# A fused attention and GEGLU kernel: new turns for its operations, other buffers for the last stores, another split of the last block

## The chip, the cores and the metric

The kernel runs on one core of a Trainium2 chip. The metric is device time in microseconds (us) of one execution; before the change the median of three runs is 225.25 us (225.17 to 226.1). Five engines work side by side, each through its own list of instructions in order: PE (TensorE, matrix products), DVE (VectorE), ACT (ScalarE), POOL (GpSimd) and SP, which here only issues DMA transfers.

## The reference

An input of 2048 rows by 448 columns, bfloat16, goes through a layer norm; an attention with memory and a gated feed-forward layer both read the result:

```python
xn = _layernorm(x, axis=-1)
s = _A_ref(xn, A_wq, A_wk, A_wv, A_wo, A_beta)
g = _silu(_B_ref(xn, B_w_gate, B_w_up, B_w_down))
return x + s * g
```

`_B_ref` is `_gelu(x @ w_gate) * (x @ w_up) @ w_down` with 1792 hidden columns. `_A_ref` has 16 heads of 28 and walks over four segments of 512 rows:

```python
for s in range(N):
    logits = jnp.einsum('bhqd,bhkd->bhqk', qs, ks) * scale + mask
    p = _softmax(logits, axis=-1)
    a_dot = jnp.einsum('bhqk,bhkd->bhqd', p, vs)
    pq = phi(qs)                       # t+1 where t>0, else exp(t)
    num = jnp.einsum('bhld,bhde->bhle', pq, M)
    den = jnp.einsum('bhld,bhd->bhl', pq, z)[..., None] + 1e-06
    outs.append(g * (num / den) + (1.0 - g) * a_dot)
    M = M + jnp.einsum('bhld,bhle->bhde', phi(ks), vs)
    z = z + jnp.einsum('bhld->bhd', phi(ks))
```

The joined outputs are multiplied by `wo`.

## The kernel before

The 2048 rows are four segments, each of four blocks of 128 rows. For a segment the kernel normalises the blocks, transposes them (in segment 0 on PE, later by DMA transposes from SP), projects q, k and v, computes scores and exponentials (sc, ex, mk), the products with v (pv), the read of the memory (rd) and its update (up). The feed-forward layer of a segment has 14 chunks of 128 hidden columns: PE computes gate and up of a chunk, ACT the GELU into one of three small buffers `gl` (line 1007), DVE the product of the two into `hT` (line 1012), which frees the two PSUM banks of the chunk for PE. Four chunks can have banks at a time. The down projection (dn), the output projection (wo), SiLU (th), the product of both (fm) and the residual (fa, line 1076) finish a block; SP stores it (st).

Segment 0 is special in three ways. Its gate and up products run in two halves, gi (through line 969, four column pieces) and gu (three pieces), where gu of a chunk has to follow the GELU of the chunk before it, or, for the first three chunks, a tiny ACT copy tg. Its q rows wait for their transposes in the slots of `hT` that chunks 8 to 11 write later, so hm08 to hm011 follow the transposes tq00 to tq03. And while its 14 chunks run, DVE also normalises segment 1 (bn, ag, ep, xn, du), and sums squares of the weights for a guard (rq).

All operations are made as named objects; a table, `TURNS`, lists all names in the order in which they are recorded, and so sets the order on every engine: a name in it is an operation, with the segment as first digit and chunk, block or step behind it (hm03: segment 0, chunk 3; st31: segment 3, block 1). The planner `arrange` checks that each name follows what it depends on and picks buffers; it changes no turn. DMA transfers go through SP in this order too, and each waits for the transfer eight before it in the program.

The last segment's blocks finish one by one: down projection, SiLU on ACT, output projection, product on DVE, residual into one of two buffers `oo`, store. The last block (b = 3) is cut in two column parts, each with its own chain; the first part's store is issued by SP, the second's by ACT. The buffer `wo_sb` of the output weights, 128 x 1792, is zeroed before the four transfers wo_in fill 28 of each 32 rows.

Of the kernel before, what the change touches and what calls it, by code (L numbers as in the profile page):

```python
# [89 lines left out]
x00 x02 x01 wv wk wv2 warm warm_up wv3 wk2 qs2 ident va0 kn0 nhalf table bn00 su2 ag00 xc0 su3 va1 wk3 wq wq2  # L90
wq3 beta wgh ez1 kn1 xc_z trc00 bn01 ag01 wuh wg0 wu0 wg4 wu4 xc2 evc00:ACT trc02 xc1 xc3 trc01 trc03 evc02:ACT
wv00 ep00 wv02 ep01 evc01:DVE evc03:DVE qs0 pw00 xn00 du00 wv03 tr00 sv3 sv2 ep03 qs3 red_z ep02 wv01 wr0 pw01
wk00 vb0 qs1 pw03 vb1 ones ez0 pw02 sq0 sq1 xn01 ev00:DVE evwv02:DVE wk02 evwv00:DVE evwv03:DVE du01 evwv01:DVE
xn03 sq2 x1 wk01 wk03 wr1 sq3 evwk02:DVE xn02 du03 evwk00:ACT evwk03:DVE wg8 evwk01:ACT wq02 wq03 du02 tr01
exwk00 ev01:DVE wq00 tr03 tr02 gates sq4 ev03:DVE wq01 wr2 ev02:DVE gi00 gi01 tk00 tk03 qs4 evwq01:ACT
evwq00:DVE evwq03:DVE evwq02:DVE wu8 tg00 exwk01 rq0 bn10 gi02 gu00 ag10 bn12 tg01 ag12 bn11 ag11 miwk01 ge00
tg02 gu01 hm00 bn13 ag13 ep10 miwk00 pw10 ge01 sq5 tq00 tq03 sq6 gi03 gu02 tk02 hm01 ge02 hm02 xn10 xn12 du10
rq1 bd bd0 tr10 gi04 gu03 ge03 gi05 gu04 ge04 xn13 hm03 gi06 du13 gu05 hm04 ge05 gi07 gu06 ge06 gi08 gu07 tr13
ge07 sq7 x2 tq01 hm05 xn11 gi09 gu08 phwk01 rq2 du11 du12 ge08 hm06 gi010 tr11 tq02 gu09 hm07 ge09 gi011 hm08
rq6 rq5 hm09 bn20 gi012 rq3 ag20 bn21 bn23 gu010 ge010 gi013 wd_in1 gu011 gu012 ge011 ag23 hm010 tk01 hm011  # L100
gu013 ge012 ge013 bd1 wk10 hm012 wk11 wr1wk0 hm013 evwk10 wo0 ag21 bn22 sc00 wq11 wd_in0 wv10 ex000 ag22 evwk11
rq4 ex001 wq10 tr12 wr1wq0 evwq10 ep20 sc01 ex010 wv11 pw20 evwq11 wr1wv0 evwv11 evwv10 sc02 xn20 xn22 xn23
ex011 mk011c384 xn21 dn000 ex020 ex021 wo_in1 mk020c0 mk021c0 bd2 mk021c256 mk001c0 sc03 mk000c0 dn005 ex030
ex031 mk031c0 mk010c0 mk011c0 x3 mk010c384 wq13 du20 phwk00 sc04 ex040 dn0010 tk10 bn30 rq7 ex041 bn31 up0 tk11
bn33 wq12 tq10 mk020c256 tq11 ag30 ag33 gates2 mk041c384 mk040c0 mk040c384 sc05 wr1wq2 macc th00 sg00 ex050
mk041c0 ex051 ag31 mk050c0 evwq13 ux tr20 bn32 exwk10 mk030c0 mk051c0 tr23 tr22 wk12 wk13 wr1wk2 evwk13 tr21
pv02 ag32 evwk12 sc06 ep30 evwq12 tq13 ex060 dn010 ex061 miwk10 sc07 dn015 ou000 ex070 pv04 sc08 phwk10 pw30
ex071 ou010 tk13 tq12 ex080 xn30 dn0110 mk060c0 dn020 th01 sc09 ex081 mk070c256 mk061c0 xn31 gx mk071c256 ex090
ex091 tk12 den000 xn32 mk071c0 mk070c0 mk060c384 xn33 du30 sg01 exwq10 den010 dn025 mk061c384 pv07 dn0210 nrm
sc10 wv12 mk080c0 bd3 mk081c0 ou020 mk090c384 tr30 ex100 ex101 den020 mk090c0 mk091c0 mk091c384 pv09 nrm2 wv13  # L110
ou030 wr1wv2 sc11 evwv12 evwv13 den030 tr31 th02 ex110 ex111 dc00 wk20 wk21 wv20 wr2wk0 mc0 miwq10 sg02 sc12
ex120 tr32 tr33 wv21 phwq10 evwk21 evwk20 wr2wv0 mk101c0 wv23 mk111c0 evwv20 wv22 wr2wv2 ex121 exwq11 sc13 dg00
dn030 rc00 evwv23 evwv22 ex130 mk110c384 rd003 mk110c0 mk120c0 mk121c256 mk121c0 mk120c256 miwq11 evwv21 rd002
rd000 rd001 wq32 rd11 wq33 wo_in0 wr3wq2 rb000 rb020 rb010 ex131 wo_in2 rb030 wo_in3 sc14 phwq11 exwk11 miwk11
mk100c0 ou111 ex140 ex141 mk140c384 evwq32 dn035 rd10 rd13 xw10 xw11 mk141c384 mk130c0 dn0310 th03 mk141c0
mk111c384 mk131c0 mk140c0 evwq33 rd12 sc15 ou101 ou131 ex150 ou121 cb00 sg03 wk22 phwk11 wk23 wr2wk2 pv12 ex151
den121 evwk22 den101 cb02 evwk23 sc16 cb01 den111 den131 ex160 ex161 wq21 wq20 up1 wr2wq0 sc17 ou100 evwq21
evwq20 pv14 wq22 tq20 tk20 den100 ou110 ex170 ex171 cb03 wq23 wr2wq2 evwq22 um1 sc18 tq22 den110 ex180 dc11
mk171c256 wo02 fm02 wo01 mk161c384 wo00 ex181 fm01 sc19 mk170c0 mk151c0 mk170c256 ex190 gu10 mk181c0 evwq23 tq23
# [1491 lines left out]
```

## Time and profile before

| what | value |
|---|---|
| median of three runs | 225.25 us (225.17 to 226.1) |
| the profiled execution's own time | 225.96 us |
| its span, first to last instruction | 224.2 us |
| granted TensorE clock | 0.997 |
| PE busy | 215.8 us, 96% of the span |
| DVE, ACT, POOL busy | 157.5, 159.7, 126.4 us |
| PE busy in the first and the last 8 us | 6.35 and 3.17 us |
| DMA | 27.71 MB, 124 GB/s on the mean |

The profile's times count from the first instruction of the span. PE's matmuls are pipelined: one of 512 columns is recorded as about 380 ns, while the next starts some 215 ns after it. So a stall of PE shows as a longer distance between two starts, and as idle time only where it is longer than the pipeline. "[0.47 <-DVE hT L1012]" behind a row means that the engine was idle for 0.47 us before it, and that this write of `hT` at line 1012 ended the wait.

### The profile page before, as it was taken

What the parts mean: (1) busy time and instruction counts of PE and PEld (TensorE: products, weight loads), DVE (VectorE), ACT (ScalarE), POOL (GpSimd) and SP (SyncE); (2) the same over time, 40 slices, a digit from 0 to 9 for tenths busy, and PEclk for the clock granted to TensorE, in tenths of its full rate; (3) what the DMA queues carried; (4) which work ended last, traced back from release to release, by engine and by line L of the source; (5) the groups of instructions that cost most, each with busy time, mean ns of one, the idle gap of its engine ahead of it and who ended that gap; (6) DMA issues with size and microseconds to landing.
All of it is one profiled execution on the core that took longest, in us unless ns stands there. A gap on an engine that the chain in (4) does not pass through costs nothing. (4 is left out here: it accounts for less than half of the span.)

```text
span 224.2 us, 5093 instructions
## 1 busy us (share of the span) xinstructions
PE 215.8 (96%) x1896; PEld 97.8 (44%) x1896; DVE 157.5 (70%) x289; ACT 159.7 (71%) x214; POOL 126.4 (56%) x219
## 2 busy tenths in 40 slices
...
GB/s 181 240 338 195 174 131 241 287 148 160 143 66 83 128 207 79 84 61 164 35 195 169 116 49 47 45 125 109 136 153 0 28 53 26 132 90 228 1 44 53
DMA packets 45463, 27.71 MB, mean 124 GB/s; under 512 B 30664, under 2 KB 40840, under 8 KB 45432
## 3 DMA queue, kind: packets, MB, share of 16 engines
...
q10 hardware_dynamic: 1216, 0.97, 1.4%
q8 instruction: 17, 0.28, 0.6%
...
## 5 line engine op out<-in xcount | busy, mean ns | idle before, releaser
L861 ACT ACTIVATE pt<-pp 128x1024 bf16<-128x1024 f32 x76 | 73.9, 1026 | 12.3 <-PE pp L846 11.9
L872 POOL TENSOR_SCALAR_AFFINE_SELECT pt<-pt 128x256 bf16<-128x256 bf16 x128 | 52.7, 445 | 13.9 <-ACT pt L861 13.6
L1055 PE MATMUL ps<-wd_sb,hT 128*128 128x448 bf16 x196 | 41.7, 353 | 0.2 <-DVE vaug L615 0.2
L1012 DVE TENSOR_TENSOR hT<-gl,ps 128x512 bf16<-128x512 bf16 x28 | 19.0, 683 | 17.6 <-ACT gl L1007 17.6
L999 PEld LDWEIGHTS <-wg_sb 64*128 64x128 bf16 x252 | 23.1, 94 | 15.1 <-issue 1.7
L999 PEld LDWEIGHTS <-wu_sb 64*128 64x128 bf16 x252 | 23.2, 94 | 14.5
L1012 DVE TENSOR_TENSOR hT<-gl,pp 128x512 bf16<-128x512 bf16 x28 | 18.6, 679 | 13.6 <-ACT gl L1007 12.5
L1055 PEld LDWEIGHTS <-hT 128*128 128x128 bf16 x210 | 19.1, 98 | 20.0 <-issue 4.2
L1007 ACT ACTIVATE gl<-ps 128x512 bf16<-128x512 f32 x28 | 16.6, 597 | 15.5 <-PE ps L999 8.4
L1007 ACT ACTIVATE gl<-pp 128x512 bf16<-128x512 f32 x28 | 16.1, 596 | 13.9 <-PE pp L999 10.2
L770 POOL TENSOR_TENSOR om<-om,rb 128x512 f32<-128x512 f32 x12 | 14.9, 1266 | 17.0 <-DMA rb<-rdr 17.0
L579 PEld LDWEIGHTS <-xnT 128*128 128x128 bf16 (+1 forms) x192 | 14.5, 96 | 21.1 <-issue 12.2
L694 POOL TENSOR_SCALAR e<-e 128x896 bf16<-128x896 bf16 (+1 forms) x12 | 11.8, 986 | 20.9 <-ACT e L689 12.5
L817 POOL TENSOR_TENSOR oT<-oa,om 128x512 bf16<-128x512 f32 x12 | 15.9, 1329 | 6.3 <-DVE oa L814 6.3
L511 POOL TENSOR_TENSOR rs<-rs,nhalf 128x1 f32<-128x1 f32 (+1 forms) x7 | 5.3, 756 | 24.3 <-DVE rs L506 24.0
L999 PE MATMUL ps<-xnT,wg_sb 64*128 64x512 bf16 x66 | 17.9, 377 | 0.0
L999 PE MATMUL ps<-xnT,wu_sb 64*128 64x512 bf16 x66 | 17.8, 376 | 0.0
L999 PE MATMUL ps<-xn,wu_sb 64*128 64x512 bf16 x66 | 17.8, 376 | 0.0
L999 PE MATMUL ps<-xn,wg_sb 64*128 64x512 bf16 x66 | 17.8, 376 | 0.0
L846 PE MATMUL pp<-qT,kT 32*128 32x384 bf16 (+3 forms) x244 | 16.5, 300 | 0.0
L999 PE MATMUL pp<-xnT,wg_sb 64*128 64x512 bf16 x60 | 16.2, 376 | 0.0
L999 PE MATMUL pp<-xnT,wu_sb 64*128 64x512 bf16 x60 | 16.2, 376 | 0.0
(132 smaller groups left out, 457.2 us busy)
## 6 DMA issues: line engine op xcount, KB each, us to landing
...
```

What stands on the lines that cost most here:

```text
L511: o = gps(f"pw{s}{bs[0]}", 0.97 if s else 0.56, lambda r=r: nc.gpsimd.tensor_tensor(out=rs.ap()[:, r], in0=rs.ap()[:, r], in1=nhalf[:, r], ...
L579: nc.tensor.matmul(out=self.bank.ap()[:, 0:D], lhsT=self.xT.ap()[r, c, n * P:(n + 1) * P], rhs=self.w[r, c, :], **kw)
L694: o = gps(f"mi{nm}{s}{half}", n / 1024, lambda: nc.gpsimd.tensor_scalar(out=t(), in0=t(), scalar1=1.0, scalar2=0.0, op0=ALU.min, op1=ALU.max),
L770: oU[s, g, 1] = t, gps(f"sm{s}{g}", 1.22, lambda t=t, r=r: nc.gpsimd.tensor_tensor(out=t.ap(), in0=t.ap(), in1=r.ap(), op=ALU.mult), deps= ...
L817: oT[s][1].append(gps(f"cb{s}{g}", 1.22, lambda g=g, t=t, tm=tm: nc.gpsimd.tensor_tensor(out=dst.ap()[:, g, :], in0=t.ap(), in1=tm.ap(), o ...
L846: nc.tensor.matmul(out=S2[i // 2].ap(i % 2)[:, c0:c0 + n], lhsT=kT[s][0].ap()[r, g, kb * P:(kb + 1) * P], rhs=qT[s][0].ap()[r, g, kb * P:L ...
L861: nc.scalar.activation(out=dst, in_=src, func=ACT.Exp, scale=scale)
L872: nc.gpsimd.affine_select(out=v, in_=v, pattern=[[0, 2], [1, P]], compare_op=ALU.is_ge, fill=0.0, base=0, channel_multiplier=-1)
L999: nc.tensor.matmul(out=bf[fc].ap(i), lhsT=w, rhs=x, start=c == 0, stop=c == 2 * NC3)
L1007: got[fc] = nc.scalar.activation(out=gl.ap(), in_=bf[fc].ap(0), func=ACT.Gelu_apprx_tanh)
L1012: nc.vector.tensor_tensor(out=hT[s][0].ap()[:, fc, :], in0=gl.ap(), in1=bf[fc].ap(1), op=ALU.mult), deps=[a] + held,
L1055: nc.tensor.matmul(out=bank.ap()[:, 0:D], lhsT=hT[s][0].ap()[:, fc, b * P:(b + 1) * P], rhs=wd_sb[:, fc, :], start=(fc == 0), stop=(fc == ...
```

## The change

Four edits, and a new table:

- `wo0`, the zeroing of `wo_sb`, moves from POOL to DVE.
- The transfer of `beta` is issued after x1 (segment 1 of the input), no longer ahead of the gate and up weights.
- In the last segment the residual sums go to the three GELU buffers `gl`, no longer to the two `oo`.
- The last block is cut at column 320, no longer at 256: 320 and 128 columns instead of 256 and 192.
- `TURNS` is replaced as a whole. On PE both tables are much alike; POOL, DVE, ACT and SP are ordered anew in many places.

```diff
@@ the table, a few of its rows @@
-fm32 wo30 dn330a wo31 dn3110 fa32:DVE fm30 dn335a dn3310a wo330 fa30:DVE dn335b dn3310b st32 th31 st30 fm31
-fa31:DVE st31 th330 y330 fa330:DVE st330 th331 wo331 y331 fa331:DVE st331
+th32 wo30 th30 fm30 wo31 dn330a wo32 st21 fa30:POOL fm31 st30 fa31:POOL st31 dn335a dn3310a wo330 dn330b dn335b
+dn3310b wo331 fm32 th330 fa32:DVE th331 st32 y330 fa330:DVE st330 y331 fa331:DVE st331
...
-        beta_in = load("SP", "beta", betac[:], A_beta.rearrange("(h o) -> h o", o=1).unsqueeze(1)
-                       .to_broadcast([H, RC, 1]), 2)
...
                 x_in[1] = [load("SP", "x1", xs[1][:], x_v[1], 448)] * NB
+                beta_in = load("SP", "beta", betac[:], A_beta.rearrange("(h o) -> h o", o=1).unsqueeze(1)
+                               .to_broadcast([H, RC, 1]), 2)
...
-        wo_z = fill("POOL", "wo0", 1.55, -70, wo_sb[:], 0.0)
+        wo_z = fill("DVE", "wo0", 0.6, -70, wo_sb[:], 0.0)
...
         def finish(s, b, pr):
-            bank, oo = Buf(B_, END if s == LAST else ONE), Buf(oo_p)
+            bank, oo = Buf(B_, END if s == LAST else ONE), Buf(gl_p if s == LAST else oo_p)
...
-            dma(f"st{s}{b}", 112, lambda: nc.sync.dma_start(out=o_v[s][:, b, :], in_=oo.ap()),
+            dma(f"st{s}{b}", 112, lambda: nc.sync.dma_start(out=o_v[s][:, b, :], in_=oo.ap()[:, 0:D]),
...
         def last_block(pr):
-            t, oo, parts, last = Buf(sg_p), Buf(oo_p), [slice(0, 256), slice(256, D)], []
+            t, oo, parts, last = Buf(sg_p), Buf(gl_p), [slice(0, 320), slice(320, D)], []
```

The first place is DVE where segment 0's chunks begin. L619 of `hT` is the eviction of a q block, L493 a bn of segment 1, L1012 a chunk's product hm, L1149 a sum of squares rq. Before:

```order
L619 TENSOR_SCALAR hT<-ps_92,rs_143 128x16x28
L1149 TENSOR_REDUCE red<-pt_108 128x16
L493 BN_STATS st_139<-x_sb_64 128x6
L495 BN_AGGR mv_142<-st_139 128x2
L493 BN_STATS st_140<-x_sb_64 128x6
L495 BN_AGGR mv_142<-st_140 128x2
L493 BN_STATS st_137<-x_sb_64 128x6
L495 BN_AGGR mv_142<-st_137 128x2
L1012 TENSOR_TENSOR hT<-gl_128,pp_91 128x512
```

With the change:

```order
L389 MEMSET wo_sb 128x896
L1149 TENSOR_REDUCE red<-pt_108 128x16
L619 TENSOR_SCALAR hT<-ps_95,rs_143 128x16x28
L619 TENSOR_SCALAR hT<-ps_93,rs_143 128x16x28
L619 TENSOR_SCALAR hT<-ps_94,rs_143 128x16x28
L493 BN_STATS st_139<-x_sb_64 128x6
L493 BN_STATS st_140<-x_sb_64 128x6
L1012 TENSOR_TENSOR hT<-gl_128,pp_90 128x512
L1012 TENSOR_TENSOR hT<-gl_129,pp_91 128x512
L493 BN_STATS st_137<-x_sb_64 128x6
```

Two bn instead of three stand ahead of the first product, and no ag; the zeroing of `wo_sb` and an rq stand ahead of the three evictions of q.

The second place is SP at the same time: transposes of k and q of segment 0, and the loads of the last gate and up columns (128x3x768). Before:

```order
L351 DMA wg_sb<-in_B_w_gate_dram 128x3x768
L628 DMA_TRANSPOSE kT_102<-kn_86 128x4x128 x2
L351 DMA wu_sb<-in_B_w_up_dram 128x3x768
L628 DMA_TRANSPOSE qT_100<-hT 128x4x128 x2
L628 DMA_TRANSPOSE kT_102<-kn_86 128x4x128
L550 DMA_TRANSPOSE xnT_99<-xn_96 128x4x128 x2
L425 DMA x_sb_65<-in_A_x_dram 128x4x448
L628 DMA_TRANSPOSE qT_100<-hT 128x4x128
```

With the change:

```order
L628 DMA_TRANSPOSE kT_102<-kn_86 128x4x128 x3
L628 DMA_TRANSPOSE qT_100<-hT 128x4x128
L351 DMA wg_sb<-in_B_w_gate_dram 128x3x768
L351 DMA wu_sb<-in_B_w_up_dram 128x3x768
L628 DMA_TRANSPOSE qT_100<-hT 128x4x128 x2
L628 DMA_TRANSPOSE kT_102<-kn_86 128x4x128
L628 DMA_TRANSPOSE qT_100<-hT 128x4x128
L550 DMA_TRANSPOSE xnT_99<-xn_96 128x4x128 x2
L425 DMA x_sb_65<-in_A_x_dram 128x4x448
```

All four transposes of q now stand ahead of segment 2's input (x_sb_65) and of those of segment 1; both weight loads stand behind four transposes instead of none and two.

The third place is DVE at the end: L1093 is fm, L1076 the residual fa, L1129 the product y of a part of the last block, L1176 the read of the guard's flag. Before:

```order
L1093 SCALAR_TENSOR_TENSOR sg_134<-sg_134,ps_95 128x448
L1076 TENSOR_TENSOR oo_136<-sg_134,x_sb_66 128x448
L1129 SCALAR_TENSOR_TENSOR sg_133<-sg_133,ps_92 128x256
L1076 TENSOR_TENSOR oo_135<-sg_133,x_sb_66 128x256
L1176 TENSOR_LOAD oki
L1129 SCALAR_TENSOR_TENSOR sg_133<-sg_133,ps_94 128x192
L1076 TENSOR_TENSOR oo_135<-sg_133,x_sb_66 128x192
```

With the change:

```order
L1093 SCALAR_TENSOR_TENSOR sg_132<-sg_132,ps_93 128x448
L1076 TENSOR_TENSOR gl_130<-sg_132,x_sb_66 128x448
L1176 TENSOR_LOAD oki
L1129 SCALAR_TENSOR_TENSOR sg_134<-sg_134,pp_90 128x320
L1076 TENSOR_TENSOR gl_128<-sg_134,x_sb_66 128x320
L1129 SCALAR_TENSOR_TENSOR sg_134<-sg_134,ps_95 128x128
L1076 TENSOR_TENSOR gl_128<-sg_134,x_sb_66 128x128
```

The residuals of blocks 0 and 1 have left DVE (they are now on POOL), the flag is read one product earlier, and the last part has 128 columns.

More of the change, by code (lines that the diff above doesn't have):

```diff
@@ L89 @@
 TURNS = """
[L90 to L119, printed above, removed]
@@ L150 @@
-ca31 dn315 ca33 st20 dn320 sm30 ca32 dn325 dn3210 th32 cb30 st23 cb31 cb33 cb32 dn300 dn305 dn3010 th30 wo32
-fm32 wo30 dn330a wo31 dn3110 fa32:DVE fm30 dn335a dn3310a wo330 fa30:DVE dn335b dn3310b st32 th31 st30 fm31
-fa31:DVE st31 th330 y330 fa330:DVE st330 th331 wo331 y331 fa331:DVE st331
+x00 x02 x01 wv wk wv2 kn1 nhalf wv3 wk2 wk3 table va1 xc_z wq warm va0 ident kn0 warm_up wq2 su2 bn00 ag00 xc0
+qs2 trc00 su3 bn01 xc2 trc02 xc3 qs4 ep00 ag01 ep01 pw00 vb1 xc1 vb0 trc03 qs0 xn00 evc00:ACT evc02:ACT du00
@@ new lines @@
+wv00 evc03:ACT trc01 pw01 evc01:DVE xn01 sv3 ep03 wv02 pw03 sv2 du01 qs1 red_z wv03 wv01 wq3 wr0 wgh wuh
+evwv00:ACT ep02 wk00 xn03 evwv01:ACT sq0 wk01 pw02 evwv02:DVE wk02 tr00 sq1 wk03 wr1 sq2 xn02 evwv03:DVE wq01
+wg0 du03 ev00:DVE evwk01:ACT wq03 evwk00:ACT evwk03:ACT rq0 wu0 evwk02:DVE qs3 bd tr01 du02 tr03 ev01:DVE wg4
+wu4 x1 beta exwk01 ev03:DVE wq02 tk00 tr02 wq00 ev02:DVE wo0 wr2 rq2 ez1 gi00 tk01 tk02 ez0 sq3 sq4 evwq01:ACT
+evwq00:DVE evwq03:DVE tq00 evwq02:DVE bn13 bn12 gi01 tg00 exwk00 gu00 gi02 tg01 ge00 gu01 gi03 miwk00 tg02 hm00
@@ new lines @@
+gu02 sq5 ge01 ge02 wg8 wu8 tq02 gi04 hm01 bn11 gu03 gi05 hm02 bn10 rq5 ag10 tq01 miwk01 ag12 ag11 ag13 ge03 gu04
+ep10 ge04 pw10 hm03 hm04 xn10 gi06 gu05 du10 xn13 ge05 du13 gi07 gu06 ge06 xn11 du11 hm05 rq1 tk03 tq03 tr10
+hm06 phwk00 xn12 gi08 tr13 gu07 ge07 gi09 gu08 ge08 sq6 hm07 hm08 rq3 x2 wo_in3 sq7 gi010 gu09 du12 ge09 gi011
+gi012 hm09 tr11 gu010 ge010 wd_in0 bd0 gi013 gu011 gu012 ge011 bn23 bn20 ag20 hm010 bn22 hm011 ge012 hm012 gu013
+ge013 hm013 wk10 wk11 wr1wk0 wo_in1 evwk10 sc00 wd_in1 tr12 evwk11 bn21 ex000 ag23 ag21 ag22 rq7 wq11 ex001 wv10
```

79 lines of the change are left out of this document (49 added, 30 removed).

## Prediction

> **What bounds the kernel now.** I first read the busy time of each engine by stretch (behind the stretch and its length: PE, PEld, DVE, ACT, POOL; then granted clock, DMA share, GB/s).
>
> ```profile
> 16.00:24.00 8.00, 7.53 (x71) 3.36 (x69) 7.12 (x18) 5.92 (x12) 3.16 (x6) 1.00 1.31 238
> 24.00:32.00 8.00, 7.87 (x72) 3.26 (x70) 7.20 (x16) 3.43 (x6) 1.83 (x2) 1.00 0.59 132
> 32.00:40.00 8.00, 7.65 (x66) 3.17 (x62) 6.88 (x14) 3.55 (x7) 0.00 (x0) 1.00 1.22 218
> 48.00:56.00 8.00, 7.72 (x84) 3.62 (x84) 7.72 (x19) 7.81 (x10) 7.67 (x19) 1.00 1.06 174
> 88.00:96.00 8.00, 8.00 (x96) 3.66 (x94) 4.02 (x9) 7.62 (x9) 4.76 (x12) 1.00 0.44 90
> ```
>
> PE is the bound. From 72 us to the end of its work (88 to 96 stands for it) it is never idle, and the others have room. So there is something to win in three places only: the chunks of segment 0 (16 to 40), the crowded attention of segment 0 behind them, where four engines are at 7.7 of 8, and the tail after PE's last product. In the first place I read PE's starts in the timeline, then what DVE, ACT, POOL and SP did there.
>
> ```profile
> 20.74 0.38 PE L969 MATMUL ps<-xnT,wg_sb 64*128 64x512 bf16 x1
> 21.59 0.37 PE L969 MATMUL pp<-xnT,wg_sb 64*128 64x512 bf16 x1 [0.47 <-DVE hT L1012]
> ...
> 21.80 0.37 PE L969 MATMUL pp<-xnT,wg_sb 64*128 64x512 bf16 x1
> ...
> 26.18 0.38 PE L969 MATMUL ps<-xnT,wg_sb 64*128 64x512 bf16 x1
> 26.68 0.37 PE L969 MATMUL ps<-xnT,wu_sb 64*128 64x512 bf16 x1
> ...
> 34.89 0.38 PE L969 MATMUL ps<-xnT,wu_sb 64*128 64x512 bf16 x1
> 35.57 0.37 PE L969 MATMUL pp<-xnT,wg_sb 64*128 64x512 bf16 x1 [0.30 <-DVE hT L1012]
> ```
>
> The starts are 0.85, 0.50 and 0.68 apart where 0.21 is the pace (21.59 to 21.80), so PE lost 0.64, 0.29 and 0.47 us: 1.40 in all, each time for a bank that hm had not freed.
>
> ```profile
> 19.06 0.60 ACT L1007 ACTIVATE gl<-pp 128x512 bf16<-128x512 f32 x1
> ...
> 18.66 0.63 DVE L493 BATCH_NORM_STATS2 st<-x_sb 128x6 f32<-128x448 bf16 x1 [0.71 <-DMA x_sb<-in_A_x_dram]
> 20.88 0.65 DVE L1012 TENSOR_TENSOR hT<-gl,pp 128x512 bf16<-128x512 bf16 x1
> 24.28 1.65 DVE L546 COPY xn<-xn 128x64 bf16<-128x64 bf16 x1
> 25.96 0.67 DVE L1012 TENSOR_TENSOR hT<-gl,ps 128x512 bf16<-128x512 bf16 x1
> 34.83 0.69 DVE L1012 TENSOR_TENSOR hT<-gl,pp 128x512 bf16<-128x512 bf16 x1 [1.04 <-DMA qT<-hT]
> ...
> 24.18 1.71 POOL L389 MEMSET wo_sb<- 128x1792 bf16 x1
> ...
> 28.50 0.58 SPq L425 DMA_DIRECT2D x_sb<-in_A_x_dram  x1
> 29.19 1.19 SPq L628 DMA_TRANSPOSE qT<-hT  x1
> ```
>
> Each stall has its own cause. The first GELU is done at 19.66, but hm00 starts at 20.88, since three bn with their ag stand ahead of it and the first of them had waited for x1. The copy at 24.28 takes 1.65 us, which ends with POOL's zeroing of `wo_sb` (25.89); the product behind it is late. And hm09 waits for tq01, which SP issued behind the load of segment 2's input.
>
> The chain of waits and the timeline show the tail:
>
> ```profile
> 216.58 2.06 DMA out_dram<-oo
> ...
> 218.44 0.62 DVE L1076 TENSOR_TENSOR oo<-sg,x_sb 128x448 bf16<-128x448 f32 x1 [0.53 <-DMA out_dram<-oo]
> 220.19 0.36 DVE L1129 SCALAR_TENSOR_TENSOR sg<-sg,ps 128x192 f32<-128x192 f32 x1 [0.34 <-DVE oo L1076]
> 220.58 0.36 DVE L1076 TENSOR_TENSOR oo<-sg,x_sb 128x192 bf16<-128x192 f32 x1
> 220.97 0.38 ACTq L1134 DMA_DIRECT2D out_dram<-oo  x1
> ...
> 216.51 1.15 PE L1113 MATMUL ps<-wd_sb,hT 128*128 128x256 bf16 x9
> 217.93 0.91 PE L1113 MATMUL pp<-wd_sb,hT 128*128 128x192 bf16 x9
> 218.67 0.49 PE L1126 MATMUL ps<-wo_sb,oT 128*128 128x192 bf16 x4
> ```
>
> PE ends at 219.16, the last residual at 220.94, 1.78 later: the residual of block 1 had waited for a store to give back one of the two `oo`, and everything on DVE behind it is late.
>
> **The tail.** Now the residuals of blocks 0 and 1 run on POOL, and with three `gl` buffers only the last block waits for a store, that of block 0, issued some 3 us ahead of PE's end E:
>
> ```profile
> L1076 POOL TENSOR_TENSOR oo<-sg,x_sb 128x448 bf16<-128x448 f32 x12 | 13.1, 1098 | 2.3 <-DVE sg L1096 2.3
> ```
>
> Counted back from E, with 0.14 us per 320-column matmul: block 0's output projection is done some 5.0 us before E, its product 0.75 later, its residual on POOL (1.10) about E-3.1; with the 2.06 us of the store the buffer is free at E-1.0. Block 1's is done on POOL by E-2.0, block 2's on DVE by E-1.3, the flag's read by E-1.1. The 320-column product starts when its projection is done, about E-1.0, and with its residual takes 0.48 + 0.50 (a line through the 192, 256 and 448-column rows), so DVE is free near E. Product and residual of the last 128 columns take about 0.30 each and can start at E+0.2: the end is E+0.85 instead of E+1.78, a gain of 0.93. It costs PE nothing by width alone: a start every 82 ns at 192 columns ((218.67-217.93)/9), 109 at 256 ((217.49-216.51)/9), so 0.42 ns per column, 55 ns at 128 and 136 at 320; 18 matmuls of each part make 3.44 us now and 3.44 then. But a floor shows here:
>
> ```profile
> L723 PE MATMUL ps<-vaug,kn 128*128 128x128 bf16 x48 | 3.2, 219 | 0.0
> ```
>
> 3.2 us over 48 is 67 ns at 128 columns, so up to +0.2; I take +0.1. Net -0.85, between -0.4 (block 0's store late by half a microsecond) and -1.05. The Trainium skill, TensorE: Matmul & The Clock Gate, section Back-to-back issue gap, speaks against the narrow part: it has 81 ns per matmul at 128 columns where weights change each time. An estimate by it: 18 x 81 ns instead of 18 x 55, +0.47, and a net tail of -0.45. The row of 67 ns is nearer to this code.
>
> **The chunks of segment 0.** Stall 1: two bn and no ag stand ahead of hm00, so it can start when x1's arrival (18.4, a little earlier without `beta` ahead) and two bn of 0.63 allow: 19.7, which is when the first GELU ends. 0.64 comes back; what is late next is DVE's later work: two more bn, an rq and four ag stand together ahead of hm03, and du and xn ahead of hm05 and hm07. Going through that order piece by piece (bn 0.63 and hm 0.67 as above, an estimated 0.2 for an ag or a du and 0.7 for an rq), hm03 and hm07 come 0.3 to 0.4 late, and the gu of chunk 3 some 0.2, for the GELU before it. Stall 2: the memset is off POOL, so nothing holds the copy: 0.29 back. On DVE it clears 896 words of four bytes, which no row shows. The nearest bound it:
>
> ```profile
> L463 DVE COPY xnT<-ps 128x512 bf16<-128x512 bf16 x4 | 1.6, 420 | 0.2
> L389 DVE MEMSET oT<- 128x64 uint32 x1 | 0.1, 112 | 0.9 <-PEq L1595 0.9
> ```
>
> The copy scaled from 512 to 896 gives 0.73, the clear of 64 words scaled to 896 gives 1.57; the second holds a fixed part 14 times, so I take 0.95. It stands in front of three evictions of q and is covered by the 2 us until their banks are wanted; without that cover it costs itself. The Trainium skill, SBUF — State Buffer, section Who interferes with whom, says that of a two-port DVE copy and a GpSimd instruction the later one is blocked until the other has ended, and that a product with a single SBUF input is not: by this the move frees this copy for good, while block 2's residual on DVE, with two SBUF inputs, could wait for POOL's in the tail; an estimate by it is up to 0.3 us, which the slack before E-1.0 covers. Stall 3: tq01 no longer stands behind segment 2's input: 0.47 back.
>
> So 1.40 is freed and I expect 0.5 of it to be lost again: -0.9, between 0 and -1.40.
>
> **The rest.** A change between full and packed matmuls costs PE about 0.09 us:
>
> ```profile
> 11.84 0.35 PE L579 MATMUL pp<-wk_sb,xnT 64*128 64x448 bf16 x1
> 12.12 1.12 PE L579 MATMUL ps<-wq_sb,xnT 128*128 128x448 bf16 x5
> ```
>
> (0.28 between starts where a pair takes 0.19). I count 125 such changes in the old PE order and 123 in the new: -0.2, or 0 where another engine sets the pace. The two gates operations of ACT, 0.19 us each, move from the idle ACT of the projections into segment 0's attention, where ACT is at 7.81 of 8:
>
> ```profile
> 14.13 0.19 ACT L443 ACTIVATE igate<-betac 128x1 f32<-128x1 bf16 x1
> ```
>
> so between 0 and +0.38; they overlap in part, and I take +0.1. The projections before 16 us hold the same matmuls in nearly the same order, and the first weights still come first: 0, plus or minus 0.3. From 72 us on PE is full, so the new order can't win there and might open a stall: 0 to +1.0; following the orders of masks, combine and read I found none and take 0.
>
> Sum: -0.85 - 0.9 - 0.2 + 0.1 = -1.85. The profiled execution has a span of 224.2 and took 225.96, above all three shown runs but the slowest (226.1); the median is 225.25. The sum applies to both: a span of 222.35, a median of 223.4.
>
> **Rivals.** *Given back:* the chunks end earlier, but segment 0's attention, with DVE, ACT and POOL near 7.7 of 8, does not start its own chains earlier, so that only the tail counts. For it speaks that row of 48 to 56; against it, that the backlog of those engines begins with the chunks' end too. 225.25 - 0.85 = 224.4, within the bound. *Late weights, slower:* the loads of the last gate and up columns now stand behind four transposes on SP:
>
> ```profile
> 10.96 0.76 SPq L351 DMA_DIRECT2D x_sb<-in_A_x_dram  x1
> 12.87 4.35 SPq L628 DMA_TRANSPOSE kT<-kn  x2
> 18.00 4.58 SPq L628 DMA_TRANSPOSE qT<-hT  x2
> ...
> 27.99 0.38 PE L969 MATMUL pp<-xnT,wg_sb 64*128 64x512 bf16 x1
> ```
>
> From 12.87, where the first is issued now, four transposes take 4.8 us at 1.2 each (as at 29.19) or 8.9 as here, and the first load 0.6; x1 took 7.7 us from issue to use (10.96 to 18.66). So the second load, issued between 18.3 and 22.4, is there between 26.0 and 30.1, or earlier if the queue is emptier by then. PE wants it for chunk 8, at 27.99 now and at 27.1 less the first two stalls. At the late end that is a stall of 3.0, and 225.25 - 1.85 + 3.0 = 226.4; it turns the sign of the sum from a landing at 28.95. *The narrow part has no effect and the table none:* if the tail's DVE chain still waits for a store and the chunks lose all again, only -0.2 + 0.1 is left: 225.15.
>
> **Chances.** Forecast (gain over 0.5%, which is 1.13 us and about what a measurement of this kernel can tell from no change): 0.60. Given back and no effect together: 0.28. Late weights or a new stall in the later segments: 0.12. For 8 in 10 the range leaves out the sum of all best cases (chunks -1.40, tail -1.05, start -0.3: 222.4) and the upper part of the late weights: 222.5 to 225.5; the forecast's own range is 222.5 to 224.1.
>
> **What would show it.** The residual of block 1 stands on POOL and nothing on DVE waits for a store; from PE's last matmul to the last residual it is some 0.85. Between 16 and 40 PE's busy time rises from 23.05 to about 23.7; hm00 follows its GELU at once; no copy of 1.6 us is left. Wrong would be a PE wait on wg_sb or wu_sb near 27, or less than 8.00 anywhere between 72 and 208.

## The result, and the profile after

The changed kernel takes 223.4 us (median of 10 runs, 222.73 to 224.22), the one before 225.21 beside it (10 runs, 224.4 to 226.26). The ratio is 0.9912 with a 95% interval of 0.9887 to 0.9938: 1.8 us faster. The forecast was 223.4. The profiled execution took 223.46 with a span of 221.7 (before: 225.96 and 224.2).

Busy time by stretch after the change, in the columns of the prediction's first fence:

```profile
16.00:24.00 8.00, 8.00 (x76) 3.42 (x74) 7.36 (x18) 5.52 (x11) 1.83 (x2) 1.00 1.22 204
24.00:32.00 8.00, 8.00 (x76) 3.20 (x74) 7.58 (x17) 4.11 (x8) 1.20 (x3) 1.00 0.99 186
32.00:40.00 8.00, 7.96 (x64) 3.19 (x61) 6.67 (x14) 4.94 (x7) 0.00 (x0) 1.00 1.02 264
48.00:56.00 8.00, 8.00 (x90) 3.47 (x88) 7.08 (x18) 7.83 (x11) 6.49 (x17) 1.00 1.05 150
80.00:88.00 8.00, 7.85 (x80) 3.45 (x74) 6.71 (x12) 6.13 (x7) 8.00 (x13) 1.00 0.75 132
176.00:184.00 8.00, 7.78 (x80) 3.16 (x80) 4.96 (x9) 6.66 (x8) 3.32 (x9) 1.00 0.08 23
```

From 16 to 40 PE is busy 23.96 us of 24 (before 23.05), and from 48 to 56 it is full too (before 7.72). Two holes are new: 0.15 us at 80.2, which the profile of the same order with the last block split at 256 (below) doesn't have, and 0.22 at 181.7, where PE waits for ACT's exponentials (the row at 181.91). The second one is in every profile with the new order in that place and in none with the old. The chunks, this hole and the tail in the timeline:

```profile
15.38 0.81 DVE L389 MEMSET wo_sb<- 128x896 uint32 x1
18.35 1.14 DVE L493 BATCH_NORM_STATS2 st<-x_sb 128x6 f32<-128x448 bf16 x2
19.74 0.69 DVE L1012 TENSOR_TENSOR hT<-gl,pp 128x512 bf16<-128x512 bf16 x1 [0.25 <-ACT gl L1007]
25.89 0.18 DVE L546 COPY xn<-xn 128x64 bf16<-128x64 bf16 x1
...
181.91 0.39 PE L846 MATMUL pp<-qT,kT 32*128 32x384 bf16 x6 [0.22 <-ACT pt L861]
...
213.19 2.03 POOL L1076 TENSOR_TENSOR gl<-sg,x_sb 128x448 bf16<-128x448 f32 x2 [3.10 <-DVE sg L1093]
215.04 0.65 DVE L1076 TENSOR_TENSOR gl<-sg,x_sb 128x448 bf16<-128x448 f32 x1
215.96 0.94 PE L1113 MATMUL pp<-wd_sb,hT 128*128 128x128 bf16 x14
216.74 0.39 PE L1126 MATMUL ps<-wo_sb,oT 128*128 128x128 bf16 x4
217.57 0.29 DVE L1076 TENSOR_TENSOR gl<-sg,x_sb 128x128 bf16<-128x128 f32 x1
217.94 0.38 ACTq L1134 DMA_DIRECT2D out_dram<-gl  x1
```

hm00 waits for its GELU alone, the copy is short, and in the tail no VectorE instruction waits for a store. PE ends at 217.13, the last residual at 217.86: 0.73 later, 1.78 before. But the execution ends at 221.7, 3.84 behind that residual, where it was 3.3 before (220.94 to 224.2). So these two traces ask two questions: E, PE's end, came 2.03 us earlier (219.16 to 217.13), more than the 0.9 that the sum gave for everything ahead of it (chunks -0.9, switches -0.2, gates +0.1, narrow part +0.1), and half a microsecond of the tail's gain was lost behind the last store.

### The profile page after: what moved, and what is told of

It reads as the page before. It is cut to its first block, busy times and chain, and to the rows that moved or that the text cites. A ratio compares the mean times of both kernels' runs of the same rounds, so it can differ in the third digit from the quotient of the medians.

```text
span 221.7 us, 5084 instructions
## 1 busy us (share of the span) xinstructions
PE 215.3 (97%) x1896; PEld 97.0 (44%) x1896; DVE 155.0 (70%) x284; ACT 159.0 (72%) x216; POOL 127.3 (57%) x220
## 4 chain that ended last, share of the span: by engine, by line
PE 87%; DVE 4%; DMA 3%; SPq 1%; issue 1%; ACT 1%; POOL 1%; ACTq 0%
PE ps L999 15%; PE ps L1055 15%; PE pp L999 13%; PE ps L579 11%; PE pp L969 6%; PE ps L1085 5%; PE pp L846 5%; PE ps L908 4%; PE ps L969 4%; PE pp L1055 2%; DMA rb<-rdr 2%; DVE vaug L615 1%; DMA x_sb<-in_A_x_dram 1%; PE ps L759 1%; SPq L787 1%
## 5 line engine op out<-in xcount | busy, mean ns | idle before, releaser
L1055 PE MATMUL ps<-wd_sb,hT 128*128 128x448 bf16 x182 | 39.0, 353 | 0.2 <-DVE vaug L615 0.2
L1012 DVE TENSOR_TENSOR hT<-gl,ps 128x512 bf16<-128x512 bf16 x29 | 19.6, 679 | 15.6 <-ACT gl L1007 15.6
L1007 ACT ACTIVATE gl<-ps 128x512 bf16<-128x512 f32 x29 | 17.1, 596 | 15.7 <-PE ps L999 9.6
L694 POOL TENSOR_SCALAR e<-e 128x896 bf16<-128x896 bf16 (+1 forms) x12 | 11.8, 986 | 23.5 <-ACT e L689 15.5
L1012 DVE TENSOR_TENSOR hT<-gl,pp 128x512 bf16<-128x512 bf16 x27 | 18.3, 683 | 7.2 <-ACT gl L1007 7.0
L817 POOL TENSOR_TENSOR oT<-oa,om 128x512 bf16<-128x512 f32 x12 | 17.1, 1434 | 2.7 <-DVE oa L814 1.9
L999 PE MATMUL ps<-xnT,wu_sb 64*128 64x512 bf16 x69 | 18.6, 377 | 0.0
L999 PE MATMUL ps<-xnT,wg_sb 64*128 64x512 bf16 x69 | 18.6, 377 | 0.0
L999 PE MATMUL ps<-xn,wu_sb 64*128 64x512 bf16 x69 | 18.6, 376 | 0.0
L999 PE MATMUL ps<-xn,wg_sb 64*128 64x512 bf16 x69 | 18.6, 376 | 0.0
L999 PE MATMUL pp<-xnT,wu_sb 64*128 64x512 bf16 x57 | 15.4, 376 | 0.0
L999 PE MATMUL pp<-xnT,wg_sb 64*128 64x512 bf16 x57 | 15.4, 376 | 0.0
L999 PE MATMUL pp<-xn,wg_sb 64*128 64x512 bf16 x57 | 15.3, 376 | 0.0
```

Of the source, the lines that this page charges most:

```text
L694: o = gps(f"mi{nm}{s}{half}", n / 1024, lambda: nc.gpsimd.tensor_scalar(out=t(), in0=t(), scalar1=1.0, scalar2=0.0, op0=ALU.min, op1=ALU.max),
L817: oT[s][1].append(gps(f"cb{s}{g}", 1.22, lambda g=g, t=t, tm=tm: nc.gpsimd.tensor_tensor(out=dst.ap()[:, g, :], in0=t.ap(), in1=tm.ap(), o ...
L999: nc.tensor.matmul(out=bf[fc].ap(i), lhsT=w, rhs=x, start=c == 0, stop=c == 2 * NC3)
L1007: got[fc] = nc.scalar.activation(out=gl.ap(), in_=bf[fc].ap(0), func=ACT.Gelu_apprx_tanh)
L1012: nc.vector.tensor_tensor(out=hT[s][0].ap()[:, fc, :], in0=gl.ap(), in1=bf[fc].ap(1), op=ALU.mult), deps=[a] + held,
L1055: nc.tensor.matmul(out=bank.ap()[:, 0:D], lhsT=hT[s][0].ap()[:, fc, b * P:(b + 1) * P], rhs=wd_sb[:, fc, :], start=(fc == 0), stop=(fc == ...
```

## The experiments

Theory: the sum of the prediction, with tail, chunks and the rest worth their terms each, and adding up. Rivals: "given back" (the attention takes the chunks' gain, so the tail is all); and one that the first trace raised, that the profiled execution of the kernel before was not a typical one. A ratio below is against the kernel before, timed beside each run on the same chip (225.07 to 225.22 us).

**The kernel before, profiled again.**

> The kernel before, unchanged, as a second profile and a measure of what the comparison can tell: ratio 1.000 with an interval of about 0.3% to each side. If the three stalls of segment 0 (0.64, 0.29, 0.47) belong to the order of the work, they are there again within 0.1 each; if the profiled execution, whose 225.96 is 0.75 above the median, was long because one of them happened to be long (the wait for the load of x1 or of segment 2's input), one of them is shorter now by about that much.

225.0 us, ratio 0.9995 (0.9972 to 1.0017). The stretches:

```profile
16.00:24.00 8.00, 8.00 (x78) 3.60 (x76) 7.62 (x18) 6.33 (x12) 3.31 (x6) 1.00 1.26 241
24.00:32.00 8.00, 7.80 (x72) 3.12 (x70) 7.23 (x15) 3.40 (x6) 1.88 (x2) 1.00 0.61 130
32.00:40.00 8.00, 7.96 (x70) 3.13 (x66) 7.41 (x15) 4.03 (x7) 0.00 (x0) 1.00 1.06 200
48.00:56.00 8.00, 7.72 (x78) 3.68 (x77) 7.72 (x19) 7.81 (x10) 7.80 (x18) 1.00 1.09 178
64.00:72.00 8.00, 7.75 (x63) 3.12 (x56) 7.92 (x15) 6.93 (x8) 5.14 (x10) 1.00 0.27 55
```

The timeline of VectorE, POOL and PE, near 25 and in the tail:

```profile
24.71 1.35 DVE L518 TENSOR_SCALAR xn<-x_sb,mv,rs 128x448 bf16<-128x448 bf16 x1
24.34 1.60 POOL L389 MEMSET wo_sb<- 128x1792 bf16 x1
...
217.38 0.62 DVE L1076 TENSOR_TENSOR oo<-sg,x_sb 128x448 bf16<-128x448 f32 x1
218.11 0.49 PE L1126 MATMUL ps<-wo_sb,oT 128*128 128x192 bf16 x4
219.53 0.36 DVE L1076 TENSOR_TENSOR oo<-sg,x_sb 128x192 bf16<-128x192 f32 x1
```

Stalls 1 and 3 are not there; only stall 2 is. In the tail the residual at 217.38 doesn't wait for a store, and the last one ends at 219.89, 1.29 behind PE's end (218.60) and not 1.78. The first execution was 0.7 us long by chance, and three of the prediction's figures (stalls 1 and 3, and the 1.78) had been read off its chance events. Seven profiles with the old tail have 1.78, 1.74, 1.46 and four times 1.29 to 1.31.

Stall 1 came with a late load: in the prediction's rows the first bn waits 0.71 us for x1. In three profiles with the same order up to there (this one, the tail alone, and attention with tail below) it doesn't wait, and PE doesn't stall. The chunks, by the first and last start of their weight loads, in the kernel before, first

```profile
L969 PEld LDWEIGHTS <-wg_sb x84: 92/94/96, 15.4 to 38.2; 64*128 64x128 bf16 x84
```

and again,

```profile
L969 PEld LDWEIGHTS <-wg_sb x84: 92/94/96, 16.0 to 37.7; 64*128 64x128 bf16 x84
```

and in the changed one:

```profile
L969 PEld LDWEIGHTS <-wg_sb x84: 92/94/96, 15.4 to 36.6; 64*128 64x128 bf16 x84
```

They last 22.8, 21.7 and 21.2 us: the change is worth 0.5 here by the middle row, 1.6 by the first. The tail alone and attention with tail (below), which have the old order up to there, take 21.7 too.

**The tail alone, and the table without the tail.** The old order up to the second half of the last gate/up stage and the new one behind it, with the new buffers and split; and the other way round.

```diff
 tail alone:   - bank, oo = Buf(...), Buf(oo_p)
               + bank, oo = Buf(...), Buf(gl_p if s == LAST else oo_p)
               - parts = [slice(0, 256), slice(256, D)]
               + parts = [slice(0, 320), slice(320, D)]
               + TURNS behind gu35: the changed kernel's
 table alone:  these lines undone; TURNS behind gu35: the old one's
```

> The kernel before with the tail of the change alone: three gl buffers for the outputs of the last segment, split at column 320, and the new order of turns from the second half of the last gate/up stage on; the order before that is the old one. By the sum (tail and rest add up): 225.2 - 0.85 = 224.35, ratio 0.996. By the rival that the chunks give their gain back in the attention, the tail is all of the change: 223.4 to 223.6, ratio 0.992 to 0.993. By what the trace of the changed kernel adds (from PE's last matmul to the last residual 0.73 instead of 1.78, but the last store lands 0.5 us later after its issue than before): -0.5, 224.7, ratio 0.998. In all cases the last residual should end 0.7 to 0.9 us after PE's last matmul.

> The changed kernel with its tail undone: outputs in the two oo buffers, split at column 256, and the old order from the second half of the last gate/up stage on; the new order before that, the zeroing on VectorE and the later load of beta stay. By the sum: 225.2 - 0.9 - 0.2 + 0.1 = 224.2, ratio 0.9956. If the three stalls come back whole and nothing is lost again (as the two traces read, 1.6 us at the end of the chunks): 223.6 to 223.8, ratio 0.993. By the rival 'given back': 225.1, ratio 0.9995. PE's last matmul should end near 217.2 as in the changed kernel, and the last residual 1.7 to 1.8 later.

The tail alone: 225.05 us, ratio 0.9995 (0.9979 to 1.0012), no gain that can be measured, though its last residual ends 0.73 behind PE's end (218.82 and 218.09). The table alone: 224.15, ratio 0.9962 (0.9935 to 0.999), -0.9; but behind the cut, where the new table passes into the old one, a wait opened that neither kernel has (timeline of POOL and PE):

```profile
208.39 2.87 POOL L817 TENSOR_TENSOR oT<-oa,om 128x512 bf16<-128x512 f32 x2 [0.63 <-DVE oa L814]
211.32 0.55 PE L1085 MATMUL ps<-wo_sb,oT 128*128 128x448 bf16 x2 [0.32 <-POOLq L1577]
```

PE stands for 0.48 us at 210.65 until POOL's oT is done at 211.26. If that wait is the cut's, the table by itself is near -1.4. Measured apart, the two halves give 0.9 of the 1.8 us; that wait is half of what is missing, and the other half isn't shown. "Given back" is refuted for the change as a whole: the tail is the small part.

**The split at 256, all else changed.**

```diff
-t, oo, parts, last = Buf(sg_p), Buf(gl_p), [slice(0, 320), slice(320, D)], []
+t, oo, parts, last = Buf(sg_p), Buf(gl_p), [slice(0, 256), slice(256, D)], []
```

> The changed kernel with the last block split at column 256 instead of 320, all else as changed. Theory: the last product and residual are of 192 columns, 0.36 each as the old trace has them, instead of 0.29 each: the end is 0.14 later from there, 223.5. The last store has 192 columns (384 bytes a row) instead of 128. If a store of 128 columns lands later than one of 192 (2.7 us from issue to landing in the changed kernel, 2.2 in the one before), the two cancel or this one is faster: 223.0 to 223.4. If the late landing is chance or comes from the order of the stores, it stays with this kernel too.

223.22 us, ratio 0.9922 (0.9898 to 0.9945): no difference to the changed kernel that can be told. From PE's end to the end of the span it is 4.41 (216.64 to 221.05) against 4.61 (217.13 to 221.74): where the block is split is worth nothing that shows.

**Pieces of the table.** The new order up to the chunks' end with the old behind it, and the old up to there with the new (and the new tail) behind it.

```diff
 chunks alone:      TURNS up to hm013 the changed kernel's, behind it the old one's, old tail
 attention + tail:  TURNS up to hm013 the old one's, behind it the changed kernel's, new tail
```

> The new order of turns up to the end of segment 0's chunks (with the zeroing on VectorE and beta after x1), then the old order and the old tail. The second profile of the kernel before showed neither stall 1 nor stall 3, and 0.36 us of stall 2; its chunks took 21.73 us from the first to the last start, the changed kernel's 21.17, and they began 0.1 to 0.8 earlier. If the gain of the chunks goes through to the end: -0.55 to -0.95, 224.1 to 224.5, ratio 0.996 to 0.9975, and the 21.17 us are there again. By the sum of the prediction (-0.9): 224.2. By 'given back' (the crowded attention behind sets its own pace): 225.0, with the chunks' end early and the first gate/up product of segment 1 not early.

> The old order (zeroing on POOL, beta at its old place) up to the end of segment 0's chunks, then the new order with the new tail. Between the chunks' end and segment 1's gate/up the second profile of the kernel before has two PE waits, 0.38 at 54.5 (a score step that waits for a bank which a VectorE eviction frees) and 0.31 at 65.2 (behind VectorE's oa), that the changed one doesn't have. If the new order of that stretch removes them by itself, from the chunks' last start to the first start of the pt x vaug products behind the first gate/up columns it takes 54.7 to 54.9 as changed, and attention and tail together are worth -0.6 and -0.4: 224.0, ratio 0.9955. If they went because the chunks ended with VectorE less behind, they are there here again, and only the tail is left: 224.7, ratio 0.998. By the sum of the prediction (tail -0.85, rest -0.1): 224.1.

Neither gains: 225.35 (1.0013, 0.9996 to 1.003) and 225.32 (1.0006, 0.9988 to 1.0024). PE's waits, first of the chunks alone, then of attention and tail:

```profile
PE ps L579 <- DVE kn L615: 1.0, 1, 1.0
```

```profile
PE ps L908 <- DVE hT L1012: 0.6, 1, 0.6
PE ps L579 <- DVE kn L615: 0.4, 1, 0.4
```

Both are inconclusive. The chunks alone are as short as in the changed kernel (15.5 to 36.7), and what they win goes at 40.0, 3 us behind the cut. But it goes to the cut: steps that the new order puts off past the chunks and the old one does within them come first behind it, and on VectorE they stand ahead of the key evictions that PE wants (its timeline):

```profile
38.55 1.08 DVE L707 SCALAR_TENSOR_TENSOR kn<-kn,e 128x896 bf16<-128x896 bf16 x1
39.55 0.61 DVE L1149 TENSOR_REDUCE red<-pt 128x16 f32<-128x448 bf16 x1
40.08 0.62 DVE L493 BATCH_NORM_STATS2 st<-x_sb 128x6 f32<-128x448 bf16 x1
...
40.69 0.59 DVE L615 CAST kn<-ps 128x448 bf16<-128x448 f32 x1
```

The other piece has an L707 of the same kind at its cut (38.93, 1.08) and the same wait, and one more at 92.2 (last section). So these two runs price neither stretch. "Given back" has to be judged by the changed kernel itself: from the chunks' last weight load to that of the last gate/up it takes 166.5 us before (37.7 to 204.2) and 166.2 changed (36.6 to 202.8), so nothing of the chunks' gain is given back. The loads for gate/up of segments 1 to 3, in the kernel before, profiled again, and in the changed one:

```profile
L999 PEld LDWEIGHTS <-wg_sb x252: 92/94/96, 87.3 to 204.2; 64*128 64x128 bf16 x126
```

```profile
L999 PEld LDWEIGHTS <-wg_sb x252: 92/94/96, 85.6 to 202.8; 64*128 64x128 bf16 x126
```

Nor does the old order take such a gain: its stretch is 166.5 to 166.6 us in four profiles whose chunks end between 36.9 and 38.2 (the kernel before twice, the tail alone, the zeroing alone). With the new order there are five more beside the changed kernel: four have 165.9 to 166.0 and one 166.4. All of the new order's gain lies ahead of segment 1's first gate/up load, which comes 49.6 us behind the chunks' end before (37.7 to 87.3), 49.0 changed (36.6 to 85.6) and 48.7 to 48.8 in those four.

**One edit each in the old order.** First the zeroing alone:

```diff
-TURNS ... evwk10 wo0 ag21 ...
+TURNS ... ev02:DVE wo0 gi00 ...
-wo_z = fill("POOL", "wo0", 1.55, -70, wo_sb[:], 0.0)
+wo_z = fill("DVE", "wo0", 0.6, -70, wo_sb[:], 0.0)
```

> The kernel before with one edit: the zeroing of the output weights' buffer on VectorE, between the evictions of segment 0's last queries and the first gate and up products, as in the change. Theory: POOL's memset held the VectorE copy of 64 columns (1.65 us instead of about 0.2), and with it stall 2, 0.29 to 0.36 us of PE near 26; both go, none of it comes back later: 224.75, ratio 0.9986. If the stall has another cause (the copy waits for its transpose, say) the long copy is there without POOL beside it. If the 0.8 us on VectorE are paid in front of PE, the start of the chunks moves by up to 0.8 and the time is 225.1 to 225.6.

224.75 us, ratio 0.9986 (0.9972 to 1.0001): the size expected, at the edge of what can be told. The stall near 26 is gone, and PE is full from 24 to 32 (7.80 in the kernel before, profiled again). But the zeroing is not free in this order. It puts VectorE's chain back by some 0.4 us, and hm00 with it (VectorE's timeline):

```profile
15.52 0.81 DVE L389 MEMSET wo_sb<- 128x896 uint32 x1
...
20.63 0.66 DVE L1012 TENSOR_TENSOR hT<-gl,pp 128x512 bf16<-128x512 bf16 x1
```

20.63 where the tail alone has 20.20, both with the chunks' first start at 15.6 to 15.7, and PE stands for 0.31 us at 20.8: stall 1, without a late load. The other way round, the changed kernel with its zeroing on POOL behind the rs step (then the timeline of POOL and VectorE):

```diff
-TURNS ... ev02:DVE wo0 wr2 ...
+TURNS ... rq1 wo0 tk03 ...
-wo_z = fill("DVE", "wo0", 0.6, -70, wo_sb[:], 0.0)
+wo_z = fill("POOL", "wo0", 1.55, -70, wo_sb[:], 0.0)
```

> The changed kernel with the zeroing back on POOL, placed so that it runs behind the rs step, near 25.2 to 26.9. Theory: the first of VectorE's three 64-column copies (25.89, 0.18 us in the changed kernel) is held until the zeroing has ended, so it lasts about 1.0 us, the two later ones stay at 0.18, and the hm behind them (27.02) comes some 0.8 later; PE waits for it for up to 0.5 us. If the long copy in the kernel before had another cause than POOL (its transpose or the loads of that time), all three stay at 0.18 and PE's time between 16 and 40 is unchanged at 23.96. The xn products ahead of the copies (0.39, two per-partition scalars and one input) may be held too, if it is not the copies alone.

```profile
24.89 1.59 POOL L389 MEMSET wo_sb<- 128x1792 bf16 x1
...
25.15 1.51 DVE L518 TENSOR_SCALAR xn<-x_sb,mv,rs 128x448 bf16<-128x448 bf16 x1
26.70 0.18 DVE L546 COPY xn<-xn 128x64 bf16<-128x64 bf16 x1
```

Not the copy is held but the product ahead of it, 1.51 us instead of 0.39, until 26.66 where the zeroing ends at 26.48; PE stands for 0.3 at 28.05. (One execution, 222.98 us, so nothing is said on its time.) In the kernel before it was the copy once (24.28) and the product once (24.71): whichever VectorE starts while POOL is at it. The cause of stall 2 is shown from both sides.

Then the eviction behind a wait of 0.3 in the attention, and as a third edit hm00 ahead of two bn:

```diff
 two moves: the zeroing as above, and
-TURNS ... evwk12 sc06 ep30 evwq12 tq13 ...
+TURNS ... evwq12 evwk12 sc06 ep30 tq13 ...
 three moves: these, and
-TURNS ... ag10 bn12 tg01 ag12 bn11 ag11 miwk01 ge00 tg02 gu01 hm00 bn13 ...
+TURNS ... ag10 tg01 miwk01 ge00 tg02 gu01 hm00 bn12 ag12 bn11 ag11 bn13 ...
```

> The kernel before with two edits: the zeroing on VectorE as in the run with that edit alone (224.75), and the VectorE eviction of segment 1's last queries (the CAST to qs at 54.38 in the second profile of the kernel before) moved ahead of a key eviction and of the rs step, so that it starts at 53.2 and the score step of 54.48 finds its bank free. Theory: the wait of 0.38 us at 54.5 goes too, and since PE sets the pace behind it nothing takes it back: 224.4, ratio 0.9968, and from the chunks' last start to segment 1's pt x vaug products 53.6 instead of 53.98. Rival: in that stretch VectorE, busy 7.7 to 7.9 of 8, is the bound; the key eviction and the rs step are now later, another wait opens within 15 us and the time stays at 224.75, 53.98 us as before.

> The two edits of the run before (zeroing on VectorE, the qs eviction earlier) and one more in the old order: hm00 ahead of the second and third bn of segment 1, so that it stands behind one bn and one ag instead of three of each. In the profiles of the old order hm00 started near 20.8 each time, and PE stood at 20.8 for 0.64, 0.49 and 0.31 us where the chunks had begun at 15.55 to 15.64, and not at all where they had begun at 16.20. Theory: hm00 starts at 19.7, when the first GELU ends, the stall is gone and the 0.3 to 0.5 us go through: 224.1 to 224.3, ratio 0.994. Rival: the bn and ag that hm00 jumped are late next, hm01 or hm03 waits behind them, PE loses the same a few us later: 224.53 as with two moves. The changed kernel stays at 223.4 either way; what is left between the two is its tail and the wait near 64, which these moves don't touch.

Two moves: 224.53, ratio 0.9955 (0.9927 to 0.9982); that is 0.2 us below the zeroing alone, and the two intervals overlap, so the second move is judged by the trace. PE's waits in the kernel before, profiled again, and with two moves:

```profile
PE ps L846 <- DVE qs L615: 0.3, 1, 0.3
PE ps L579 <- DVE oa L744: 0.2, 1, 0.2
```

```profile
PE ps L579 <- DVE oa L744: 0.4, 1, 0.4
PE pp L969 <- DVE hT L1012: 0.3, 1, 0.3
```

The wait for qs is gone, and the next one, 10 us on, grew by 0.1: the larger part went through. Stall 1 is in this execution too (the row of L969, 0.49 us, with hm00 at 20.78 behind the zeroing), and the third move aimed at it. (The expectation lays stall 1 to the chunks' start; the rows show a late load in one case and the zeroing in the others.) The move made things worse: 224.91, ratio 0.9987 (0.9968 to 1.0005). VectorE's timeline there:

```profile
19.70 0.69 DVE L1012 TENSOR_TENSOR hT<-gl,pp 128x512 bf16<-128x512 bf16 x1 [0.51 <-ACT gl L1007]
...
22.70 0.68 DVE L1012 TENSOR_TENSOR hT<-gl,pp 128x512 bf16<-128x512 bf16 x1
```

and among PE's waits

```profile
PE pp L969 <- DVE hT L1012: 0.8, 1, 0.8
```

hm00 starts at 19.70 as in the changed kernel, but the bn and ag it jumped stand together ahead of hm01, which starts at 22.70 (20.78 in the changed kernel), and PE waits 0.8 for that. The rival held: in the changed kernel the four bn are spread, two ahead of hm00, one behind hm01 and one behind hm02, which by the rows makes room for hm00 and for the zeroing; no run tried that spread of the bn by itself.

**The end of the program.** The changed kernel with two `oo` for three `gl`, and with one store for the last block:

```diff
-bank, oo = Buf(B_, END if s == LAST else ONE), Buf(gl_p if s == LAST else oo_p)
+bank, oo = Buf(B_, END if s == LAST else ONE), Buf(oo_p)
```

> The changed kernel, its order and its split unchanged, but the last segment's outputs in the two oo buffers instead of the three of gl. Theory of the tail: the residual of block 2 then waits for the store of block 0 and that of the last block for the store of block 1, both landing about 2.5 us after their issue; going through the new order on VectorE the last residual ends some 0.9 us later than with three buffers, E+1.6 to E+1.8: 224.0 to 224.3, ratio to before 0.996, that is 0.6 to 0.9 over the changed kernel. If the end is set by something else than the last residual (the landing of the last stores beside other traffic), the loss is 0 to 0.3: 223.4 to 223.7.

VectorE in that run:

```profile
216.93 0.63 DVE L1076 TENSOR_TENSOR oo<-sg,x_sb 128x448 bf16<-128x448 f32 x1 [1.83 <-DMA out_dram<-oo]
```

With two buffers and the new order, 223.99 (0.9954, 0.9939 to 0.997), 0.6 over the changed kernel: block 2's residual waits 1.83 us for block 0's store. The buffers do what was said. But that doesn't compare the new tail with the old one, whose order is another and waits less.

```diff
-op(f"st{s}{b}{h}", {"ACT" if h else "SP": (0.6, 1.7)}, lambda h=h, r=r: (nc.scalar if h else nc.sync).dma_start(
-    out=o_v[s][:, b, r], in_=oo.ap()[:, r]), deps=[o], prio=pr, uses=[oo], kb=n / 4)
+op(f"st{s}{b}", {"SP": (0.6, 1.7)}, lambda: nc.sync.dma_start(
+    out=o_v[s][:, b, :], in_=oo.ap()[:, 0:D]), deps=[o], prio=pr, uses=[oo], kb=D / 4)
```

> The changed kernel with the last block's output in one store of 448 columns, issued by SP behind the last residual, instead of a store of 320 and one of 128 columns; nothing else moves. In all profiles with the new tail (the changed kernel, the tail alone) the two last stores land 2.7 us after their issue, with the last 16th of the 320-column one 1.0 to 2.4 us behind its first, where the old ones needed 2.2, and this is where the gain of the residual went. If two small stores close behind each other are the reason, one of 448 columns lands 2.1 to 2.3 after its issue at about E+0.85: the end comes 0.3 to 0.5 earlier, 222.9 to 223.1. If the landing is held by other traffic at the end (instruction fetches of the engines), a larger store is as late or later: 223.4 to 224.0. If PE's own end is what holds it (its first instruction behind the last matmul comes 3.2 us after it, 0.3 us ahead of the last landing in the changed kernel) the gain is at most 0.3.

223.54 (0.9902, 0.9865 to 0.9939), the same. The idea that two small stores get in each other's way is not borne out: the one large store, issued at 217.69, lands from 219.20 to 220.44, 2.75 us after its issue. From the issues and the landing records of the traces (us; PE's end is that of its last matmul):

```
                 PE's end   last residual   last store   last       span's
                            ends            issued       landing    end
before            219.16     220.94          220.97       223.16     224.24
before again      218.60     219.89          219.92       222.46     223.54
two moves         217.73     219.03          219.06       221.97     223.05
table alone       217.18     218.92          218.95       221.12     222.20
tail alone        218.09     218.82          219.21       221.52     222.86
changed           217.13     217.86          217.94       220.66     221.74
split at 256      216.64     217.50          217.58       219.91     221.05
one store         216.93     217.66          217.69       220.44     221.58
attention, tail   218.52     219.25          219.64       222.74     223.84
```

(At 256 the last landing is that of the first part's store.) The last landing is 2.2 to 2.9 us after the last issue with the old tail and 2.3 to 3.1 with the new. From PE's end to the span's end it is 4.74 to 5.32 in seven profiles with the old tail, 4.99 in the mean, and 4.35 to 5.32 in six with the new one and three buffers, 4.69 in the mean: the tail is worth some 0.3, with a scatter as large. In two of the six, the tail alone and attention with tail, the last store is issued 0.39 us behind the last residual instead of 0.03 to 0.08; what held it isn't shown. The other four have 4.51 in the mean, so the tail may be worth 0.5 in the changed kernel, and the run of the tail alone may have shown too little.

## Why the prediction was right, and where it was right by luck

The time was right to 0.1 us, and the sum behind it was not. By its own steps:

- **The tail, -0.85: mis-sized, about -0.3.** Its mechanism came out step by step: residuals of blocks 0 and 1 on POOL in one piece, no wait for a store, last product and residual 0.29 each, the end at E+0.73 where 0.85 was said. The step that failed is "E+0.85 instead of E+1.78, a gain of 0.93". The 1.78 was one execution's, in which a store landed late; most old ones have 1.30. And the gain was counted to the last residual, as if what lies behind it were constant: the store's landing scatters by as much as the gain. Counted to the end of the span, 0.3 is left (0.5 without the two late issues), and the tail alone measured 0.9995.
- **The narrow part, +0.1: nothing.** The 14 starts from 215.96 on are 56 ns apart ((216.74 - 215.96)/14), what the line through the wider rows gave (55). The floor of 67 ns belongs to the row of L723 and not to these matmuls. The 81 ns that the Trainium skill gives for a sustained stream (TensorE: Matmul & The Clock Gate, Back-to-back issue gap) are not borne out; the formula that the same section keeps for a single matmul, N/2.4 + 2.5 ns, gives 56, which is the stream's pace here.
- **The chunks, -0.9: about -0.5, with some -0.1 from an earlier start.** (The first start in PE's timeline is 15.5 to 15.7 in six of the seven profiles with the old order and 16.2 in the seventh, 15.3 to 15.7 with the new: without the one of 16.2 the means are 0.1 apart.) Of the 1.40 that was to be freed only stall 2 (0.29 in the first trace, 0.36 in the others) is in all four profiles that have the old order and its zeroing. Stall 3 is in none but the first, and so is stall 1, in the one where x1 came late. "0.5 lost again" didn't happen in the changed kernel. The zeroing was costed at nothing, under "2 us until their banks are wanted"; its cover is not that but the place of hm00: in the old order it costs 0.3 to 0.5 there.
- **The rest, -0.1: about -0.5.** This is the step that failed for want of a look: the profile's 7.72 from 48 to 56 and its 7.75 from 64 to 72 were two waits of PE, 0.38 at 54.5 and 0.3 at 65.2 in the second profile, in the stretch the prediction named as one of three to win in and then priced with mode switches alone. The new order has neither; for the first it was shown that one eviction in front is enough. Mode switches and gates can't be told beside that. The stretch ahead of segment 1's first gate/up load is 0.6 to 0.8 us shorter, about what the two waits make, and the hole at 181.7 takes 0.2 of it back.
- **From 72 us on, 0:** right within 0.2 to 0.4, and not as it was said: the sign of being wrong, "less than 8.00 anywhere between 72 and 208", came twice (7.85 and 7.78). The hole at 181.7 belongs to the new order, in which following the orders of masks, combine and read had found no stall; the hole at 80.2 is in this one profile alone.
- **Given back:** refuted for the change, by the same stretch.
- **Late weights:** no wait on `wg_sb` or `wu_sb`, and PE is full from 24 to 32. Refuted.
- **"The sum applies to both":** it was taken that the 0.7 by which the profiled execution lay above the median lay outside the terms. It lay in them: the late x1, the wait for tq01 and the late store are what made that execution long.

So -0.1 for the start, -0.5, -0.5 and -0.3 make -1.4 of the 1.8 measured; the single executions these are read from scatter by 0.3, and the remaining 0.4 is not settled. Two errors met: the tail and the chunks were too large by 0.95, the attention and the start too small by 0.5.
